# A second DMA queue for later weights and tokens, and a new instruction order, in an attention and feed-forward kernel

## The chip, the cores and the metric

The kernel runs on one core of one Trainium2 chip. The metric is the device time of one execution in microseconds, as the median of several executions. The engines are called by the profile's names: PE (TensorE, matrix products), DVE (VectorE), ACT (ScalarE), POOL (GpSimd) and SP (SyncE, which only issues DMAs here). A DMA is issued by an instruction on SP, POOL or ACT, and its packets are moved by 16 DMA engines. Packets of SP's issues show as queue q1 (hardware), those of POOL's as queue q0 (software).

## The reference

Eight batches of 512 tokens with 8 heads of 64, and 32 state rows per batch and head. Tokens read the state and the state reads the tokens, each by attention; both results together (544 rows of 512 for each batch, 4352 rows in all) go through a feed-forward layer with a gate.

```python
scores  = scale * x @ state.T;  a  = softmax(scores);   xread = a @ state
scores2 = scale * state @ x.T;  a2 = softmax(scores2);  sread = a2 @ x
z = concatenate([xread, sread], axis=2)          # (8, 8, 544, 64), then rows of 512
h = z @ w_in                                     # w_in 512 x 2048
g = h * clip(h + 3, 0, 6) / 6
out = g @ w_out                                  # w_out 2048 x 512
```

The weights arrive in eight bytes per number; the kernel loads them so and puts a 32-bit number together from the two halves.

## The kernel before

**Units and steps.** The feed-forward layer is cut along its width of 2048 into 16 tiles of 128, numbered 0 to 15. A *unit* is one pass of eight tiles over one batch, and each tile in it is a *step*. The first sweep takes tiles 0 to 7: units 0 to 7 for the batches' tokens, unit 8 for the state rows of all batches (`sread`). The second sweep takes tiles 8 to 15: unit 9 for the state rows, units 10 to 17 for the tokens. A step makes `h` for its tile (`first(n)`, tile `ps_h`), ACT and DVE turn it into `g` (L1286, L1289), split it into a high and a low part (`g_hi` on ACT, `g_lo` on DVE, L396 and L397) and PE adds three products of them to the accumulators (`second(n)`, tiles `acc`). Products are made of such high and low parts throughout, so that three fast products stand for one exact one. The first sweep's partial output is written to `out` in HBM (`put_out`, L1350); in the second sweep it is added there by an accumulating DMA from POOL (L1176).

**The attention of the next batch** is spread over the steps of the current unit. For batch b its state is loaded by POOL in four block DMAs (`load_state`, L547), its tokens are loaded a second time in a block order that makes DVE's 32 x 32 transposes into a full one (`load_turned`, L611, 16 issues of 512 pieces for each batch, on SP), and a third time by rows (`load_x`, L582, tile `xb`, four issues of 1024 pieces of 256 bytes, on SP). The softmax of the states is moved between partitions by 16 small DMAs (`weights_moved`, L964, "raw<-raw", on SP). PE reads `xb` and the moved weights in `tokens_read` (L992). There is one `xb` buffer, so a batch's tokens go in after the batch before has been read. POOL also stores each batch's attention weights for the second sweep (`keep`, L1387, L1391).

**Weights.** `weight(kind, k, ...)` loads w_in or w_out tile k (L473), ACT converts the upper halves to `tops` (L484, L486), DVE joins the halves (L491), and for w_out ACT and DVE split the result (L518, L520). Tiles 0 to 7 are loaded at the head. Tiles 8 to 15 are loaded one at a time into `raw`, a ring of three buffers that the turned tokens and the moves use as well; the second sweep is the first to use them. All these loads are issued by SP.

**What sets the order.** Every instruction is entered into a `Plan` with its engine, a cost, its readers and writers. `Plan.order` places all of them with a list scheduler that takes, on each engine, the instruction with the smallest number in `RANKS` among those that could start within 0.3 us; the code is then issued in that order, and each engine works through its own list in order. So an instruction that waits holds up whatever stands behind it on its engine. Of a DMA the plan takes the transfer at 330 bytes per ns over one channel, a landing time of 1.4 us and an allowance `late`:

```python
done = channel + self.LANDING + late
...
def Q(rank, size, do, reads=(), writes=(), after=(), pieces=128, cost=0.46, late=2.0):          # SP
def by_pool(rank, size, do, reads=(), writes=(), after=(), pieces=128, cost=1.3, late=3.0):     # POOL
...
for f in range(FPS, NF):                      # tiles 8 to 15
    told = 16.0 + 5.0 * (f - FPS)             # the step from which the load is entered
    weights.append((told, "in", f, 1, ("raw", ("in", f)), told + 4, told + 4))
    weights.append((told + 2, "out", f, 1, ("raw", ("out", f)), told + 6, told + 6))
```

`first_of[n]` is the plan's number of the first product of step n; other entries use it as "not before step n".

Of the kernel before, what the change touches and what calls it, by code (L numbers as in the profile page):

```python
# [17 lines left out]
ALU = mybir.AluOpType  # L18
# [255 lines left out]
def tile_state_attention_then_hardswish_ffn(  # L274
# [87 lines left out]
    def by_pool(rank, size, do, reads=(), writes=(), after=(), pieces=128, cost=1.3, late=3.0):  # L362
        return plan.add("P", cost, rank, do, reads, writes, after, size, pieces, late)
# [211 lines left out]
    def load_x(b, rank, after=(), read=False):  # L575
# [3 lines left out]
        if b:  # L579
            for j in range(J):  # L580
                def load(j=j):
                    nc.sync.dma_start(x_tile(b, read)[:, :, j, :], x_v[b, j])  # L582
# [975 lines left out]
```

## Time and profile before

| what | value |
|---|---|
| median of 3 runs | 650.12 us (648.83 to 651.21) |
| the profiled execution | 647.97 us, of which the span from first to last instruction is 646.2 us |
| PE busy | 633.2 us (98%) |
| DVE busy | 509.9 us (79%) |
| ACT busy | 326.2 us (50%) |
| POOL busy | 53.5 us (8%) |
| granted clock of PE | 1.000 over the whole span |
| packets of SP's queue | 133248, 46.47 MB, 31.1% of 16 engines' span |
| packets of POOL's queue | 9328, 25.63 MB, 16.1% |

The profile is of one execution, so its rows add up to its own time and not to the median. Times in rows are microseconds from the span's start unless marked ns. A matrix product is shown from its start to its end, and products overlap: the next starts 0.23 us after one that is shown as 0.39 long. So PE counts as busy while one is in flight, and an idle gap in the rows is shorter than what the stop costs. "<-" after an idle time names what ended it, by the semaphores' events.

### The profile page before, as it was taken

How to read it: one execution, taken by the hardware profiler on the slowest of the kernel's cores; microseconds unless marked ns; L12 is line 12 of the kernel's file. 1: busy time of each engine (PE TensorE's matmuls, PEld its weight loads, DVE VectorE, ACT ScalarE, POOL GpSimd, SP SyncE). 2: the span in 40 equal slices, each digit the busy share in tenths (PEclk: the TensorE clock that was granted, in tenths of full speed). 3: DMA queues.
4: the chain of work that ended last, by engine and by line, in shares of the span. 5: the costliest groups of instructions: out<-in, count | busy, mean ns of one | idle time of the engine just before them, and what ended most of it. 6: DMA issues, size and time to landing. Idle time of an engine off the chain costs nothing.

```text
span 646.2 us, 11490 instructions
## 1 busy us (share of the span) xinstructions
PE 633.2 (98%) x4444; PEld 518.2 (80%) x4444; DVE 509.9 (79%) x937; ACT 326.2 (50%) x587; POOL 53.5 (8%) x82
## 2 busy tenths in 40 slices
PE   8999989999999999999999999999999999999997
PEld 6566667877776868778899878898989898998996
DVE  5989679888977869786578758888787887897773
ACT  5966444654645454535446545455454364445431
POOL 2200202011020201001000000000000000000000
PEclk9999999999999999999999999999999999999999
DMA  8994796958659478344201031241433341341232
GB/s 295 309 210 92 196 181 148 228 129 188 149 126 209 112 212 172 105 77 146 67 22 66 2 106 66 33 102 23 96 51 83 49 105 22 85 66 16 46 71 66
DMA packets 142774, 73.09 MB, mean 113 GB/s; under 512 B 120896, under 2 KB 130176, under 8 KB 142592
## 3 DMA queue, kind: packets, MB, share of 16 engines
q1 hardware_dynamic: 133248, 46.47, 31.1%
q0 software_dynamic: 9328, 25.63, 16.1%
q8 instruction: 35, 0.57, 0.4%
q10 hardware_dynamic: 144, 0.26, 0.1%
q14 instruction: 19, 0.16, 0.1%
HBM read 42.45 MB, written 26.21 MB: 106 GB/s over the span
## 4 chain that ended last, share of the span: by engine, by line
PE 85%; DMA 5%; DVE 5%; SPq 2%; ACT 2%; issue 1%; DVEq 0%
PE ps_h L1035 28%; PE acc L1035 27%; PE acc L1147 24%; PE ps_s L624 3%; SPq L611 2%; PE ps_h L624 2%; DMA raw<-raw 1%; DMA raw<-in_moe_w_in_dram 1%; DMA early<-in_moe_w_out_dram 1%; DMA raw<-in_moe_w_out_dram 1%; PE ps_h L992 1%; PE acc L1318 1%; PE ps_s L787 1%; DMA st_raw<-in_state_dram 1%; PE acc L723 0%
## 5 line engine op out<-in xcount | busy, mean ns | idle before, releaser
L1035 PE MATMUL acc<-w_out_hi,g_hi 128*128 128x512 f32 x296 | 117.2, 396 | 0.3 <-ACT g_hi L396 0.3
L1035 PE MATMUL acc<-w_out_hi,g_lo 128*128 128x512 f32 x296 | 115.5, 390 | 1.4 <-DVE g_lo L397 1.3
L1035 PE MATMUL acc<-w_out_lo,g_hi 128*128 128x512 f32 x296 | 115.5, 390 | 0.0
L1147 PE MATMUL acc<-w_out_hi,tmp 128*128 128x256 f32 x360 | 89.1, 283 | 0.0
L1035 PE MATMUL ps_h<-aT_hi,wp_hi 128*128 128x512 f32 (+1 forms) x228 | 84.5, 371 | 1.9 <-DVE ot L397 1.4
L1286 ACT ACTIVATE g<-ps_h,three 128x512 f32<-128x512 f32 (+1 forms) x80 | 50.8, 646 | 64.8 <-PE ps_h L1035 55.3
L1035 PE MATMUL ps_h<-aT_lo,wp_hi 128*128 128x512 f32 (+1 forms) x228 | 82.4, 361 | 0.0
L1035 PE MATMUL ps_h<-aT_hi,wp_lo 128*128 128x512 f32 (+1 forms) x228 | 82.0, 360 | 0.0
L1270 ACT ACTIVATE G<-ps_h,three 128x512 f32<-128x512 f32 x64 | 44.2, 690 | 67.2 <-PE ps_h L1035 65.9
L1035 PEld LDWEIGHTS acc<-w_out_hi,g_hi 128*128 128x128 f32 x296 | 55.6, 188 | 19.3 <-issue 6.7
L1289 DVE SCALAR_TENSOR_TENSOR g<-g,ps_h 128x512 f32<-128x512 f32 (+1 forms) x80 | 49.6, 630 | 26.0 <-ACT g L1286 25.6
L1147 PE MATMUL acc<-w_out_hi,g_hi 128*128 128x256 f32 x240 | 68.4, 285 | 0.0
L1147 PE MATMUL acc<-w_out_lo,g_hi 128*128 128x256 f32 x240 | 67.9, 283 | 0.0
L1147 PE MATMUL acc<-w_out_hi,g_lo 128*128 128x256 f32 x240 | 67.9, 283 | 0.0
L1147 PEld LDWEIGHTS acc<-w_out_hi,tmp 128*128 128x128 f32 x360 | 66.8, 192 | 1.3 <-issue 0.8
L1035 PEld LDWEIGHTS acc<-w_out_hi,g_lo 128*128 128x128 f32 x296 | 55.6, 188 | 14.5 <-DVE g_lo L397 2.7
L1035 PEld LDWEIGHTS acc<-w_out_lo,g_hi 128*128 128x128 f32 x296 | 55.6, 188 | 10.6
L396 ACT CAST g_hi<-g 128x512 fp32r<-128x512 f32 (+1 forms) x74 | 42.3, 584 | 37.3 <-DVE g L1289 19.9
L1272 DVE SCALAR_TENSOR_TENSOR G<-G,ps_h 128x512 f32<-128x512 f32 x64 | 43.8, 685 | 17.6 <-ACT G L1270 17.0
L397 DVE TENSOR_TENSOR g_lo<-g,g_hi 128x512 fp32r<-128x512 f32 (+1 forms) x74 | 46.8, 642 | 13.0 <-ACT g_hi L396 12.1
L1035 PEld LDWEIGHTS ps_h<-aT_hi,wp_hi 128*128 128x128 f32 x228 | 43.1, 189 | 10.9 <-DVE ot L397 2.3
L1147 PEld LDWEIGHTS acc<-w_out_hi,g_hi 128*128 128x128 f32 x240 | 45.9, 191 | 6.7 <-ACT wp_hi L396 1.7
(169 smaller groups left out, 1209.8 us busy)
## 6 DMA issues: line engine op xcount, KB each, us to landing
out_dram<-ot POOLq DMA_DIRECT2D x8, 1024.0 KB, 5.8
out_dram<-ot POOLq DMA_DIRECT2D x15, 512.0 KB, 5.9
raw<-in_x_dram SPq DMA_DIRECT2D x112, 64.0 KB, 3.2
xb<-in_x_dram SPq DMA_DIRECT2D x28, 256.0 KB, 5.0
raw<-in_moe_w_out_dram SPq DMA_DIRECT2D x11, 511.8 KB, 7.1
raw<-in_moe_w_in_dram SPq DMA_DIRECT2D x8, 511.0 KB, 4.6
raw<-raw SPq DMA_DIRECT2D x112, 32.0 KB, 2.0
early<-in_moe_w_in_dram SPq DMA_DIRECT2D x3, 1023.0 KB, 10.3
```

What stands on the lines that cost most here:

```text
L396: first = S_(cost, rank, lambda: nc.scalar.copy(hi(), src()), reads, [writes[0]], after)
L397: V(cost, rank, lambda: nc.vector.tensor_tensor(lo(), src(), hi().bitcast(F32), op=ALU.subtract), [*reads, writes[0]], [writes[1]])
L611: nc.sync.dma_start(t[rows, i].rearrange("t (a c) -> t a c", c=NS), x[b, 4 * g + 2 * i + u, :, k * NS : (k + 1) * NS].rearrange("(a t) c - ...
L624: nc.tensor.matmul(out[u][cols, :], made["stT", b][rows, cols], moving(q)[rows], start=True, stop=True,)
L787: nc.tensor.matmul(out[:, j, q % 2], xT(b, q)[:, j * P : (j + 1) * P], apart[:, q], start=True, stop=True,)
L992: nc.tensor.matmul(bank(pr)[cols, u * D : (u + 1) * D], e2T(b, u)[:, j * P + q * NS : j * P + (q + 1) * NS], x_tile(b, True)[:, NG * q + u ...
L1035: nc.tensor.matmul(ps, l, r, start=start and k == 0, stop=stop and k == n - 1)
L1147: nc.tensor.matmul(out, left(a, l), right(b, r), start=p == 0 and z == 0 and y == 0, stop=p == FPS // 2 - 1 and y == 2, skip_group_check=True)
L1270: S_(0.68, n - 1.5, lambda: nc.scalar.activation(g(), by_pass(), AF.Relu, bias=three, scale=-1.0 if turned_sign(FPS + i) else 1.0), [ps], ...
L1272: V(0.63, n - 1.5, lambda: nc.vector.scalar_tensor_tensor(g(), g(), 6.0, by_pass(), op0=ALU.min, op1=ALU.mult), [ps], [g_key])
L1286: in_turn["g", n] = S_(cost + 0.05, rank, lambda: nc.scalar.activation(g(), bank(ps)[:, :width], AF.Relu, bias=three, scale=-1.0 if turned ...
L1289: V(cost, rank, lambda: nc.vector.scalar_tensor_tensor(g(), g(), 6.0, bank(ps)[:, :width], op0=ALU.min, op1=ALU.mult), [ps], [g_key])
```

## The change

- The loads of weight tiles 8 to 15 are issued by POOL and not by SP, and each gets a condition: not before the first product of the step three before the one at which it is entered. (`first_of` now holds step numbers alone, and is made earlier in the code; the list kept in it under "sums" moves to `sum_of["all"]`.)
- The token loads by rows of batches 1 to 7 (`load_x`) are issued by POOL and not by SP.
- The first sweep's output store of a unit becomes four stores, one for each 128 rows, each waiting for its own part of `ot`. What reads the stored rows later (the accumulating stores, `load_part`) waits for the parts that it needs.
- The plan's cost of a POOL issue goes from 1.3 to 0.65, that of a batch's four state loads from 4.8 to 2.4; a token load on POOL is given 1.5. POOL's weight loads get the allowance `late` of 3.0 where SP's had 2.0.
- `RANKS` is new in full (the list differs in length, as there are more instructions), so the order on every engine can differ anywhere.
- Turned loads, moves, the loads of tiles 0 to 7, of batch 0, and the reloads of the second sweep stay on SP.

```diff
@@ RANKS: replaced in full
...
-    def by_pool(rank, size, do, reads=(), writes=(), after=(), pieces=128, cost=1.3, late=3.0):
+    def by_pool(rank, size, do, reads=(), writes=(), after=(), pieces=128, cost=0.65, late=3.0):
...
-            nc.sync.dma_start(flat[:, :, : flat.shape[2] - 1], src)
+            (nc.gpsimd if k >= FPS else nc.sync).dma_start(flat[:, :, : flat.shape[2] - 1], src)
...
-        Q(load_rank, 524.288 * n, load, writes=[key], pieces=128 * n if kind == "out" else 512,
-          late=2.0 if k >= FPS else 0.5)
+        pieces_of = 128 * n if kind == "out" else 512
+        if k >= FPS:
+            by_pool(load_rank, 524.288, load, writes=[key], after=[first_of[max(first_of) - 2]],
+                    pieces=pieces_of)
+        else:
+            Q(load_rank, 524.288 * n, load, writes=[key], pieces=pieces_of, late=0.5)
...
-        by_pool(rank, 140.0, load_blocks, writes=[key], after=after, pieces=512, cost=4.8)
+        by_pool(rank, 140.0, load_blocks, writes=[key], after=after, pieces=512, cost=2.4)
...
-                    nc.sync.dma_start(x_tile(b, read)[:, :, j, :], x_v[b, j])
-                Q(rank, 420.0, load, writes=[(*key, j)], after=after, pieces=1024, cost=0.55)
+                    nc.gpsimd.dma_start(x_tile(b, read)[:, :, j, :], x_v[b, j])
+                by_pool(rank, 420.0, load, writes=[(*key, j)], after=after, pieces=1024, cost=1.5)
...
-            [*[(*o_key, 2 * q + r) for r in range(2)], ("part", units[k][1])], [], (), 1000.0, 256, 3.0)
+            [*[(*o_key, 2 * q + r) for r in range(2)], *[("part", units[k][1], 2 * q + r) for r in range(2)]], [], (), 1000.0, 256, 3.0)
...
-          [("part", units[k][1])], [("po", k, j) for j in range(2, J)], after, pieces=256)
+          [("part", units[k][1], j) for j in range(2, J)], [("po", k, j) for j in range(2, J)], after, pieces=256)
...
-            by_pool(n + 3, 262.0 * nt, lambda: nc.gpsimd.dma_start(rows_of(b), ot()), keys, [("part", b)], pieces=512)
+            for j in range(nt):
+                by_pool(n + 3, 262.0, lambda j=j: nc.gpsimd.dma_start(rows_of(b)[:, j], ot()[:, j]),
+                        [keys[j]], [("part", b, j)])
```

## Rows read from the trace of the kernel before

**Rows 1.** The windows by stage: the stretch and its length, then for each engine its busy time and its instructions, the granted clock of PE (1.00 is full), the mean busy share of the 16 DMA engines, and GB/s.

```profile
0.00:20.00 20.00, 16.78 (x156) 14.32 (x156) 13.33 (x29) 11.35 (x23) 4.20 (x12) 1.00 0.89 314
20.00:60.00 40.00, 39.05 (x280) 23.17 (x278) 37.69 (x69) 30.09 (x57) 3.86 (x7) 1.00 0.79 180
100.00:200.00 100.00, 99.88 (x698) 77.09 (x697) 86.52 (x158) 53.17 (x93) 13.85 (x24) 1.00 0.70 165
220.00:285.00 65.00, 65.00 (x475) 49.58 (x474) 48.64 (x83) 31.97 (x55) 3.28 (x6) 1.00 0.58 139
390.00:642.00 252.00, 252.00 (x1845) 225.14 (x1829) 199.83 (x376) 119.47 (x224) 17.48 (x15) 1.00 0.31 62
20.00:642.00 622.00, 616.43 (x4290) 503.93 (x4288) 495.86 (x908) 314.88 (x566) 49.26 (x70) 1.00 0.47 107
```

**Rows 2.** The windows of four narrow stretches of the first sweep, in the same columns (PE, its weight loads PEld, DVE, ACT, POOL, clock, DMA share, GB/s).

```profile
56.00:62.00 6.00, 5.14 (x85) 3.83 (x84) 5.97 (x12) 4.64 (x8) 0.74 (x2) 1.00 0.28 64
75.00:83.00 8.00, 6.48 (x96) 3.76 (x94) 5.33 (x9) 3.79 (x6) 0.00 (x0) 1.00 0.42 73
92.00:98.00 6.00, 5.01 (x45) 2.82 (x30) 5.59 (x12) 3.52 (x7) 0.00 (x0) 1.00 1.02 175
205.00:210.00 5.00, 3.58 (x16) 2.64 (x15) 4.77 (x10) 3.36 (x7) 0.00 (x0) 1.00 0.92 149
```

**Rows 3.** The waits of PE between 20 and 646, longest first: the waiting tile and line, what it waited for, us in total, times, longest.

```profile
PE ps_h L1035 <- DVE ot L397: 1.4, 1, 1.4
PE acc L1035 <- DVE g_lo L397: 1.3, 2, 0.9
PE ps_h L992 <- DMA raw<-raw: 0.8, 1, 0.8
...
```

**Rows 4.** Three links of the chain of work that ended last, from the stretches 62 to 97 and 195 to 212: start, us, what.

```profile
69.41 9.22 DMA raw<-raw
84.46 7.09 DMA raw<-in_moe_w_in_dram
...
197.39 5.68 DMA raw<-in_moe_w_out_dram
```

**Rows 5.** The timelines of ACT and DVE at the conversions of three later weights: start, us, engine, line, operation, tiles, and in brackets the engine's idle time before and what ended it.

```profile
75.98 0.78 ACT L486 CAST tops<-raw 128x512 f16<-128x512 bf16 x1 [2.34 <-DMA raw<-in_moe_w_out_dram]
91.58 0.80 ACT L484 ACTIVATE tops<-raw 128x512 f16<-128x512 bf16 x1 [0.85 <-DMA raw<-in_moe_w_in_dram]
203.09 0.78 ACT L486 CAST tops<-raw 128x512 f16<-128x512 bf16 x1 [0.45 <-DMA raw<-in_moe_w_out_dram]
76.79 0.69 DVE L491 SCALAR_TENSOR_TENSOR raw<-raw,tops 128x512 uint32<-128x512 uint32 x1 [2.43 <-ACT tops L486]
```

**Rows 6.** The timeline of PE, in the same columns: the start of step 15, the read of batch 2's tokens, and the stop near 207.

```profile
96.33 0.50 PE L1035 MATMUL ps_h<-aT_hi,wp_hi 128*128 128x512 f32 x1
...
111.96 0.26 PE L992 MATMUL ps_h<-xb,raw 128*32 128x64 f32 x4
...
206.55 0.39 PE L1035 MATMUL acc<-w_out_lo,g_hi 128*128 128x512 f32 x1
206.78 0.39 PE L1035 MATMUL acc<-w_out_hi,g_lo 128*128 128x512 f32 x1
208.59 0.50 PE L1035 MATMUL ps_h<-aT_hi,wp_hi 128*128 128x512 f32 x1 [1.42 <-DVE ot L397]
```

**Rows 7.** The timeline of SP, which issues DMAs: start, us that SP spent on it, tiles.

```profile
68.82 0.54 SPq L473 DMA_DIRECT2D raw<-in_moe_w_out_dram  x1
...
84.46 0.99 SPq L473 DMA_DIRECT2D raw<-in_moe_w_in_dram  x1
...
93.30 0.49 SPq L582 DMA_DIRECT2D xb<-in_x_dram  x1
```

**Rows 8.** The DMA issues of the whole span: tiles, issuing engine, count, KB of each, median us from issue to landing.

```profile
out_dram<-ot POOLq DMA_DIRECT2D x8, 1024.0 KB, 5.8
...
xb<-in_x_dram SPq DMA_DIRECT2D x28, 256.0 KB, 5.0
raw<-in_moe_w_out_dram SPq DMA_DIRECT2D x11, 511.8 KB, 7.1
...
raw<-raw SPq DMA_DIRECT2D x112, 32.0 KB, 2.0
...
out_dram<-ot SPq DMA_DIRECT2D x3, 256.0 KB, 2.9
```

**Rows 9.** POOL's DMA issues by source line: ns that one takes on POOL as least/median/most, first and last start; and from the same view of L1387 the time that POOL sat idle before the keeps and what ended it (us, times). A store of L1350 has 512 pieces (batch 0's 128), a keep of L1387 and a state load of L547 have 128.

```profile
L1350 POOL DMA_DIRECT2D out_dram<-ot x8: 562/767/767, 69.5 to 339.3; - x8
...
L1387 POOL DMA_DIRECT2D a2hi<-aT_hi x1: 555/555/555, 104.0 to 104.0; - x1
...
  ACT aT_hi L396: 166.5, 8
...
L547 POOL DMA_DIRECT2D st_raw<-in_state_dram x28: 552/554/1047, 6.2 to 219.5; - x28
```

**Rows 10.** The first part of the page: busy time, share of the span and instructions of each engine.

```profile
PE 633.2 (98%) x4444; PEld 518.2 (80%) x4444; DVE 509.9 (79%) x937; ACT 326.2 (50%) x587; POOL 53.5 (8%) x82
```

**Rows 11.** The DMA queues between 20 and 60: packets, MB, and the time that their packets took, as a share of 16 engines over the 40 us.

```profile
q1 hardware_dynamic: 18619, 5.99, 70.1%
q0 software_dynamic: 448, 1.18, 8.6%
```

More of the change, by code (lines that the diff above doesn't have):

```diff
@@ L533, in tile_state_attention_then_hardswish_ffn @@
     wp_at, scores_at, turned_first = {}, {}, {}
+    first_of, in_turn = {}, {}
     def load_state(b, rank, after=()):
@@ L1036, in product @@
                 k += 1
-    first_of, in_turn = {}, {}
     whole_of, sum_of = {}, {}
@@ L1097, in quarter_sums @@
         wide, half = (0.34, 0.21) if last else (0.6, 0.34)
-        if "sums" not in first_of:
-            first_of["sums"] = [m for slot, users in plan.users.items() for m in users
+        if "all" not in sum_of:
+            sum_of["all"] = [m for slot, users in plan.users.items() for m in users
                                 if slot[0] in ("ot", "top", "sread", "apart")]
@@ L1103, in quarter_sums @@
             to(0, 2), four()[:, :, 1:3], four()[:, :, 0:1].to_broadcast(list(four()[:, :, 1:3].shape)),
-            op=ALU.subtract), g_keys, [s_keys[0]], first_of["sums"] + chain)
+            op=ALU.subtract), g_keys, [s_keys[0]], sum_of["all"] + chain)
         V(half, rank, lambda: nc.vector.tensor_tensor(
@@ L1161, in seconds @@
         S_(0.36, rank, lambda: nc.scalar.mul(E()[:, left_half], bank(acc[0])[:, left_half], -1.0 / 6.0),
-           [acc[0]], [e_key], first_of["sums"])
+           [acc[0]], [e_key], sum_of["all"])
         def join(cost, out, a, b, reads, writes):
```

205 rows, old and new, of the table RANKS are left out of this document.

## The prediction

> **What bounds the kernel now.** I read the windows first. TensorE (PE) is busy 616.43 of the 622 us between 20 and 642, at full clock throughout [rows 1]; what a change of queues can win there is PE's 5.57 us of idle and what each restart costs. Ahead of 20 PE lacks 3.2 us. From 390 to 642 it is busy 252.00 of 252.00: the second sweep has nothing to win and can only lose. From 20 to 60 VectorE (DVE) is busy 37.7 of 40 us, so what little PE misses there is elementwise work, not a queue.
>
> Then I cut the first sweep more finely to find the idle [rows 2]: 0.86 at 56 to 62, 1.52 at 75 to 83, 0.99 at 92 to 98, 1.42 at 205 to 210; the other 0.78 is spread. The list of who waited for whom names DVE tiles for most of it [rows 3], but DVE is only the last link. The chain of work and the timelines of ACT and DVE show the first link of the three large ones [rows 4, 5]:
> - At 92 to 98 the chain runs through the load of a later w_in tile, issued at 84.46 and 7.09 us under way. ACT's conversion (L484) stands in ACT's order at 91.58 and waits for it; DVE's join, the moves' transposes and then `g_lo` follow, and PE idles 0.99.
> - At 205 to 210 the same with a w_out tile: issued 197.39, 5.68 us, ACT's conversion at 203.09, then a row of DVE work in fixed order, and PE starts at 208.59 after 1.42 [rows 6].
> - At 75 to 83 a w_out tile issued at 68.82 [rows 7] holds ACT for 2.34 (75.98) and DVE for 2.43 (76.79) [rows 5]. Besides, a move raw<-raw issued right behind it on SP, at 69.41, needs 9.22 us where the median is 2.0 [rows 4, 8], and 0.8 us of PE's idle is a wait for such a move [rows 3].
>
> So 1.52 + 0.99 + 1.42 = 3.93 us of idle hang on three of the sixteen loads of weights with number 8 and up. PE wants none of these weights before the second sweep; they hurt because ACT and DVE take their conversions in a fixed order, among work that PE wants now. A stop costs more than its idle: from 206.78 to 208.59 there are 1.81 us between two starts that are 0.23 apart otherwise, so 1.58 is lost for 1.42 idle, 0.16 for the restart [rows 6]. I count five stops at the three places, three of them in the first, 0.8 us. Together **4.7 us**.
>
> **The change, part by part.** *Later weights to GpSimd (POOL).* Sixteen issues leave SP. What matters more is the new condition: a load added at step n may not be issued before the first product of step n-3. With the ranks in the code (16 + 5 per tile, w_out two later) the first may go at step 13, the second only at step 15, the last at step 50. Step 15 starts at 96.33 [rows 6]; today both loads of 68.82 and 84.46 are issued before that [rows 7]. So two of the three guilty loads leave the place where DVE is busy 5.97 of 6 and 5.59 of 6 us [rows 2], and their DVE work, 0.69 for each join [rows 5], with them. It is done later, where DVE is busy 86.5 of 100 and 48.6 of 65 us [rows 1]. The third falls in with a plan that allows a POOL load 3.0 us beyond transfer and landing, where it allowed an SP load 2.0: 1.6 + 1.4 + 3.0 = 6.0 us instead of 5.0, against a median of 7.1 for a w_out tile and the 5.68 of the guilty one [rows 4, 8]. Between no gain (other loads become late instead) and the full 4.7, I take the removal of all three.
>
> *Given back.* Three loads of sixteen stop PE today. In the new order the moved loads meet a DVE as full as at 100 to 200 at first and emptier later; from 220 to 285, where the last of them go, PE is now busy 65.00 of 65.00 with DVE free a quarter of the time [rows 1]. Between none and three new stops, I count one of the mean size, 3.93/3 + 0.16 = **1.5 us**.
>
> *Tokens of batches 1 to 7 to POOL.* 28 issues. On POOL no load of 1024 pieces is shown. The nearest: 128 pieces take 555 ns (keep, L1387) and 512 pieces 767 (store, L1350) [rows 9], 0.55 ns a piece, which makes 1.05 us; bounds 0.55 (as for 128) and 1.53 (in proportion to the pieces). 28 x 1.05 = 29 us, on an engine that is busy 53.5 of 646 us [rows 10] and off the path. What hides a later landing: of batch 2 the last part is issued at 93.30 [rows 7], lands 5.0 us later in the median [rows 8] and is read at 111.96 [rows 6]. That is 13 us of cover; when it is gone, PE waits at L992 for each us beyond. In the DMA engines the loads should become cheaper: between 20 and 60 POOL's queue shows 448 packets [rows 11] for 896 pieces issued there (two keeps of 128, one state of 128, four state loads of 128 each), so it joins small pieces. Its packets took 8.6% of 640 us for 1.18 MB, 47 us a MB, and SP's 70.1% for 5.99 MB, 75 us a MB; 7.3 MB of tokens so cost 343 instead of 548, 13 us of all 16 engines. The moves left on SP gain from that and from no longer queueing behind tokens; I book nothing, as the 0.8 us that PE waits for a move is counted above. Were the small packets of SP and POOL's large ones to get in each other's way instead, the same 13 us of cover stands in front of it.
>
> *Output stores in four parts.* 32 issues of about 0.55 for 8 that take 5.9 in all [rows 9]: 17.6 - 5.9 = 11.7 us more on POOL. A part of 256 KB lands in 2.9 us, the whole in 5.8 [rows 8], so the `ot` tile comes free up to 3 us sooner. No PE wait is put down to a store: worth 0. The finer keys of the accumulating stores, a sweep later, change nothing.
>
> *Cheaper POOL costs and the new order.* Costs of 0.65 and 2.4 are the plan's figures and act through the order alone. Where nothing is idle an order gains nothing; I book 0, with the idle left, 5.57 - 3.93 = 1.6, as the upper bound of a gain. POOL grows by 29 (tokens), 8 x 0.77 + 8 x 0.55 = 10.6 (weights) and 11.7 to 105 us.
>
> Sum: 4.7 - 1.5 = 3.2. The profiled execution took 647.97 with a span of 646.2; it would take 644.8. It lies 2.15 below the median of the three runs, 650.12, and I carry the difference over: **646.9**.
>
> **A rule against it.** POOL's state loads take 552 ns at least and 554 in the median, and 1047 once [rows 9], in stretches in which DVE is busy 87 to 94% of the time [rows 1]. The Trainium skill (SBUF — State Buffer, "SBUF: two separate sides") says that a DVE instruction in a two-port mode locks GpSimd out, so that it can't write descriptors and its DMAs look blocked by DVE. The trace agrees at most in that one issue; were it the rule here, the gain would fall to nothing, by the third rival.
>
> **Rivals.**
> 1. *The stop moves.* Three of the moved loads, or of the moves, stop PE elsewhere: 4.7 - 3 x 1.5 = 0.2 gained, 649.9. For it: a fixed order with a DVE as full as in rows 1 leaves little room. Against: the condition on the steps, and PE without idle from 220 to 285. Chance 0.22.
> 2. *POOL's order blocks: slower.* POOL's keeps of `aT_hi` wait for ACT, 166.5 us in eight waits [rows 9]. A load ordered behind such a wait is as late as ACT is, and its conversion stops ACT and DVE in turn: 1.5 us in each of up to seven batches. From five on (7.5 - 4.7 = 2.8) it is slower, 652.9; with seven, 655.9. Against: tokens are issued 13 us and more before they are read, and the order can place them ahead of the keep. Chance 0.16.
> 3. *POOL's issues stretch.* With 1047 for 554 ns the six moved loads of a unit end 3 us later in turn, and the three stops stay: 650.1. This is what the rule would do. Chance 0.03.
> 4. *More than forecast.* No new stop, and the order takes the remaining 1.6 too: 650.12 - 4.7 - 1.6 = 643.8. Chance 0.09.
>
> **How the numbers follow.** The forecast has 0.50, from no new stop (645.4) to nearly two (648.1); that is its own range. A difference of 0.3%, 2 us, is about what a measurement of this kernel can tell from none. Below 648.2 lie the forecast and rival 4: 0.59 faster. Rivals 1 and 3: 0.25 same. Rival 2: 0.16 slower. The range goes down to 642.0 (all idle of 20 to 642, 5.6, with 1.4 for its restarts, and 1.1 of the 3.2 us at the head) and up to 653.5, which takes in rival 2 with five stops.
>
> **What would show it.** Right: at most one later weight issued before 96; no ACT wait of over 0.5 us for a later weight; PE idle in 20 to 642 down from 5.6 to about 2.5; token loads near 1.05 us each on POOL; POOL near 105 us; far fewer packets on POOL's queue than 28 x 1024 for the tokens. Wrong: PE idle at L992 on tokens, POOL issues of several us, idle after 390, or the same idle behind other DVE instructions.

## The result and the profile after

The changed kernel takes 655.67 us in the median of 14 runs (652.16 to 659.14), the kernel before 650.75 us beside it on the same chip: a ratio of 1.0077, interval 1.0049 to 1.0104. It is slower by 5 us, where 646.9 and faster was forecast. The profiled execution of the changed kernel took 652.16 us, with a span of 650.4. When the changed kernel was timed again beside other experiments, one of ten executions took 2200 us; without it the median of that repeat is 655.35 and not 656.14.

The windows after, in the columns of [rows 1]:

```profile
20.00:80.00 60.00, 59.45 (x442) 39.97 (x441) 52.82 (x95) 38.35 (x69) 14.14 (x23) 1.00 0.74 184
80.00:100.00 20.00, 16.85 (x94) 11.45 (x93) 15.55 (x32) 8.35 (x17) 3.52 (x4) 1.00 0.70 109
100.00:200.00 100.00, 99.25 (x693) 76.82 (x693) 85.32 (x156) 52.08 (x92) 34.46 (x54) 1.00 0.80 182
200.00:220.00 20.00, 14.68 (x81) 9.85 (x80) 11.75 (x20) 7.54 (x13) 1.33 (x2) 0.91 0.45 85
...
390.00:642.00 252.00, 252.00 (x1861) 225.52 (x1861) 203.62 (x383) 121.84 (x228) 17.43 (x15) 1.00 0.30 61
```

PE lacks 0.55 us between 20 and 80, and then 3.15 and 5.32 us in two stretches of 20 us; the second sweep is as full as before. Products counted in the two timelines of PE say the same: the 201st product of 512 columns starts at 81.7 us after and at 85.8 before, so the change is 4.1 us ahead there. At the 701st it is 4.6 behind (223.1 and 218.5), and so it stays to the end. The two orders put the smaller products at different places, so the count is a rough measure: in idle time alone the lead at 80 is 1.3 us (0.55 for 1.84).

The longest wait of PE, which answers to [rows 3], and the longest wait of DVE for a load (us, times, longest):

```profile
PE acc L1041 <- DVE g_lo L398: 8.4, 3, 5.3
...
DVE tmp L720 <- DMA raw<-in_x_dram: 10.8, 4, 7.0
```

DVE's timeline at the two places:

```profile
91.46 0.71 DVE L720 STREAM_TRANSPOSE tmp<-raw 128x512 f32<-128x512 f32 x1 [3.29 <-DMA raw<-in_x_dram]
...
206.66 0.71 DVE L720 STREAM_TRANSPOSE tmp<-raw 128x512 f32<-128x512 f32 x1 [6.96 <-DMA raw<-in_x_dram]
207.30 0.65 DVE L398 TENSOR_TENSOR g_lo<-g,g_hi 128x512 fp32r<-128x512 f32 x1
```

A transpose of the next batch's turned tokens stands in DVE's order ahead of `g_lo`, which PE wants at once. It waits 6.96 us for a load, and `g_lo` waits behind it. The links of the chain of work there (start, us, what), which answer to [rows 4]:

```profile
83.70 7.73 DMA raw<-in_x_dram
...
198.07 8.57 DMA raw<-in_x_dram
```

Both are turned loads, which the change leaves on SP. The timelines of SP and POOL show what was issued beside them:

```profile
78.69 13.79 SPq L617 DMA_DIRECT2D raw<-in_x_dram  x16
80.08 3.52 POOL L588 DMA_DIRECT2D xb<-in_x_dram  x4 [7.96 <-PE ps_h L998]
...
189.70 16.97 SPq L617 DMA_DIRECT2D raw<-in_x_dram  x16
190.77 0.90 POOL L588 DMA_DIRECT2D xb<-in_x_dram  x1 [1.59 <-PE ps_h L998]
196.77 1.76 POOL L588 DMA_DIRECT2D xb<-in_x_dram  x2
```

The tokens now go out while the turned loads do, 1.4 and 1.1 us behind the first of them, as soon as a product (L998) has read the batch before. Beside the second stop POOL also issues one w_in and one w_out tile (188.41 and 196.22) and four small state loads. Before, SP put tokens and turned loads in a row, as its timeline shows:

```profile
190.54 6.17 SPq L611 DMA_DIRECT2D raw<-in_x_dram  x7
...
198.23 0.43 SPq L611 DMA_DIRECT2D raw<-in_x_dram  x1
198.70 5.35 SPq L582 DMA_DIRECT2D xb<-in_x_dram  x4
206.04 4.04 SPq L611 DMA_DIRECT2D raw<-in_x_dram  x8
```

The DMA queues of the changed kernel between 189 and 207 (packets, MB, share of 16 engines), and the landing of turned loads there:

```profile
q0 software_dynamic: 656, 2.16, 51.5%
q1 hardware_dynamic: 7574, 0.94, 45.6%
...
raw<-in_x_dram SPq DMA_DIRECT2D x16, 64.0 KB, 6.5
```

The 16 engines are full, and POOL's queue (q0) has more than half of their time while the urgent loads, on q1, take the rest. Of the 2.16 MB on q0 the tokens are 1.05 and the two weight tiles as much, so this view alone does not say which of them costs; the experiments do.

### The profile page after: what moved, and what is told of

The parts are those of the page before. It is cut to its first block, busy times and chain, and to the rows that moved or that the text cites. A ratio compares the mean times of both kernels' runs of the same rounds, so it can differ in the third digit from the quotient of the medians.

```text
span 650.4 us, 11556 instructions
## 1 busy us (share of the span) xinstructions
PE 633.3 (97%) x4440; PEld 517.9 (80%) x4440; DVE 510.2 (78%) x937; ACT 325.7 (50%) x587; POOL 99.7 (15%) x150
## 4 chain that ended last, share of the span: by engine, by line
PE 82%; DVE 5%; SPq 5%; DMA 5%; issue 1%; ACT 1%; DVEq 0%
PE ps_h L1041 26%; PE acc L1041 25%; PE acc L1152 23%; PE ps_s L630 3%; SPq L970 3%; DMA raw<-in_x_dram 3%; PE ps_h L630 2%; SPq L617 2%; DMA raw<-raw 1%; PE acc L1323 1%; DMA early<-in_moe_w_in_dram 1%; PE ps_h L998 1%; DVE tmp L720 1%; ACT tops L487 0%; DVE nm L897 0%
## 5 line engine op out<-in xcount | busy, mean ns | idle before, releaser
L1181 POOL DMA_DIRECT2D out_dram<-ot x15 | 17.4, 1162 | 275.2 <-DVE ot L1170 275.2
```

Source lines behind the costliest of these rows:

```text
L1181: plan.add("P", 1.3, rank, lambda: nc.gpsimd.dma_start(rows_of(units[k][1])[:, 2 * q : 2 * q + 2], ot_of(k)[:, 2 * q : 2 * q + 2], accum_o ...
```

## The experiments

Each is timed beside the kernel before on the same chip (650.5 to 651.1 us). Two theories stood at the outset. A: the tokens on POOL starve the turned loads on SP. B: the new order itself is at fault.

**Parts undone, one at a time.** Changed kernel; the first with the tokens' line back on SP, the second with the weights' line, the third with both:

```diff
-  nc.gpsimd.dma_start(x_tile(b, read)[:, :, j, :], x_v[b, j])
+  nc.sync.dma_start(x_tile(b, read)[:, :, j, :], x_v[b, j])
...
-  (nc.gpsimd if k >= FPS else nc.sync).dma_start(flat[:, :, : flat.shape[2] - 1], src)
+  nc.sync.dma_start(flat[:, :, : flat.shape[2] - 1], src)
```

> The changed kernel with the token loads of batches 1 to 7 issued by SP again, at the places that the new order gives them; everything else as changed. Theory A (POOL's packets of up to 4 KB and more share the DMA engines with SP's turned loads of 128-byte packets; a turned load beside them lands after 7 to 9 us, and the DVE transposes stop PE): the two stops behind L720 (2.7 and 5.3 us) go or shrink to under 1.5 together, DVE's waits for turned loads fall from 10.8 to under 4 us, and the time falls by 4 or more to 649 to 652. Theory B (the new order itself asks for the turned loads too early, whoever carries the tokens): the waits stay at 8 or more and the time at 654 to 658.

> The changed kernel with the loads of weights 8 to 15 issued by SP again, new order kept. Theory A: tokens stay on POOL beside the turned loads, so most of the lateness stays; 0.5 MB a weight now queues in front of turned loads on SP instead: 653 to 657. Theory B: also about 655, since the order is unchanged. This run separates the two parts of the move, not the theories.

> The changed kernel with tokens and weights both issued by SP again, new order and four-part stores kept. Theory A: with only stores and keeps left on POOL in the first sweep, turned loads land as before (median 3 to 4 us): 648 to 652. Theory B: 655 or more, because the order was made for two queues and now everything waits in one.

Measured: tokens on SP 645.76 us, ratio 0.9937 (0.9902 to 0.9972), faster than both kernels and than the 649 to 652 of theory A; weights on SP 654.07, 1.0063 (1.0041 to 1.0085); both on SP 650.01, 0.9998 (0.9967 to 1.0030). The new order and the four-part stores alone are worth nothing, so B falls in its plain form. Under this order, with the tokens on SP, the weights on POOL gain 650.01 - 645.76 = 4.2 us in the medians (2.4 to 3.2 when like executions are compared, as the last section shows), and with the weights on POOL the tokens there cost 655.67 - 645.76 = 9.9. Taken the other way round, the tokens on POOL cost 654.07 - 650.01 = 4.1 with the weights on SP, and the weights on POOL then gain nothing: 655.67 with them, 654.07 without, and the intervals of the two ratios overlap. So the effects do not add in this order.

**The same parts alone, in the old order.** Kernel before with only the tokens' line on POOL, only the weights' line, or both (the edits above, turned round).

> The kernel before, in its own order, with only the issue of the token loads of batches 1 to 7 moved to POOL. Theory A: turned loads issued beside the tokens land later (median from 3.2 to over 4 us), DVE's waits for them rise from 1.9 to 6 or more, and the time rises by 2 to 6 us to 653 to 657. Theory B: within 2 us of the kernel before, 649 to 652.

> The kernel before, with its own order and whole stores; only the weight loads from number 8 on are issued by POOL. Theory A (what costs time is the tokens' large packets beside SP's turned loads; the weights on POOL help): between 645.5 and 648.5 us for 650.8 before, as the weights were worth 4.2 us in the new order (650.01 against 645.76); ACT's waits for w_in and w_out under half of the 12.1 us of before. Theory B (POOL's queue hurts whatever it carries): 652 or more, with DVE waiting for turned loads (L714) more than 4 us. Theory C (the weights are worth something only in the new order): 649 to 651.

> The kernel before, with its own order and whole stores; both the weights from number 8 on and the tokens of batches 1 to 7 are issued by POOL. If the two effects add as they do in the new order (weights -4.2, tokens +9.9 to +12.1): 656 to 659 us. If the new order of the changed kernel had taken back part of the tokens' price, this kernel is slower than the changed one's 655.7 by 2 us or more. If they do not add, since SP's queue is freed of both: 651 to 655.

Measured: tokens 662.90, ratio 1.0198 (1.0154 to 1.0242), more than either theory had; weights 649.04, 0.9994 (0.9971 to 1.0016); both 650.14, 0.9998 (0.9964 to 1.0033). The tokens alone cost 12.1 us, which speaks against B. But it is not the wait that A named: DVE waits 3.0 us for turned loads, where A had 6 or more. Of the other two, the weights came out as theory C had it, and both together as none of the three expectations did: the effects do not add here either, and in the old order both parts together cost nothing. The waits of ACT in the run with the tokens alone name what was late there:

```profile
ACT tops L484 <- DMA raw<-in_moe_w_in_dram: 14.2, 2, 7.2
```

There the w_in loads, still on SP and behind turned loads that crawl, are late: the one issued at 84.24 lands after 12.45 us, where the kernel before took 7.09 [rows 4]. With the weights on POOL too, this victim is gone. So the tokens on POOL slow whatever SP's queue holds then, and the order decides whether somebody waits for it. DVE's timeline in the run with both shows the old order's choice:

```profile
217.35 1.28 DVE L714 STREAM_TRANSPOSE tmp<-raw 128x512 f32<-128x512 f32 x2
```

The old order asks for batch 6's turned tokens at 217.35, and there they wait for nothing; the new one asked at 206.66 - 6.96 = 199.70, when the last load of that transpose was 1.63 us old (198.07). In the numbers by which `Plan.order` places things (no times of the chip), that load stands 23.9 us ahead of the transpose in the old order and 5.2 in the new. At the first stop these times are alike (6.3 and 6.4 us). What differs at both is how many loads the first transpose must wait out: in the old order it needs the 4th and the 5th of the batch's 16 turned loads, in the new one the 9th and the 11th.

**Is it POOL's packets or any second queue?** Changed kernel with the tokens on ACT's queue, which moves them in packets of 256 bytes (29264 packets for 7.60 MB; the same loads add 2240 packets to POOL's queue); and a kernel of DMAs alone.

```diff
-  nc.gpsimd.dma_start(x_tile(b, read)[:, :, j, :], x_v[b, j])
+  nc.scalar.dma_start(x_tile(b, read)[:, :, j, :], x_v[b, j])
```

> The changed kernel, but the tokens of batches 1 to 7 are issued by ACT's queue instead of POOL's: still another queue than SP's, at the same time as the turned loads, but in packets of 256 bytes rather than POOL's 4096. Theory A1 (the size of the other queue's packets starves SP's packets of 128 bytes): the turned loads land near 4 us in the median, DVE's wait for them under 3 us, total 645 to 650 (ACT pays 28 issues of some 0.05 to 0.1 us, and what it queues behind them). Theory A2 (any second queue beside the turned loads starves them): DVE waits 7 us or more, 654 to 658. Theory A3 (ACT's order suffers: its token issue waits for the buffer that TensorE frees, and the work behind it on ACT is late): over 652 with waits of PE on ACT's g_hi and little wait of DVE for turned loads.

Measured: 656.73 us, ratio 1.012 (1.0061 to 1.0179). DVE's wait:

```profile
DVE tmp L720 <- DMA raw<-in_x_dram: 13.3, 4, 6.3
```

As slow as with POOL, and DVE waits as long for turned loads: A1, which blamed the size of POOL's packets, falls, and A2 holds in the main. A3 may have a share that was not separated: ACT stands 5.0 us before two `g_hi` until a token load lands, and an issue takes ACT 0.37 us at least, not 0.05 to 0.1. The kernel of DMAs alone:

```python
def phase(b, beside, tiles):    # DVE writes a corner of every tile: all loads start together
    for t in (turned[0][:, 0, 0:2], turned[1][:, 0, 0:2], *tiles):
        nc.vector.memset(t, 0.0)
    beside()                    # nothing; tokens on POOL, ACT or SP; two w_out tiles on POOL or ACT
    load_turned(b)              # the 16 turned loads of a batch on SP
    close(...)                  # DVE reads a corner of every tile
```

> A kernel that leaves out the whole computation and writes zeros: eight phases, each the 16 turned loads of one batch on SP (1 KB rows of 128-byte packets), released together with one other set of loads: 0 nothing, 1 tokens on POOL, 2 tokens on ACT, 3 tokens on SP behind nothing, ahead of the turned loads, 4 two w_out tiles on POOL, 5 two w_out tiles on ACT, 6 tokens on POOL again, 7 nothing again. Time from the first issue to the last landing of the turned loads. Theory A1: phases 0 and 7 about 12 to 14 us (16 issues of some 0.6 us and a landing of 3), phases 1 and 6 at least 4 us more, phase 2 less than 2 us more, phase 4 up to 4 us more. Theory A2: phases 1, 2, 4, 5, 6 all at least 3 us more. If the cost needs the rest of the kernel (theory D: the starving comes from moves and other traffic): all phases within 2 us of phase 0. Times of whole phases say nothing on the kernel before.

Its windows for phase 0 (nothing beside), 1 (tokens on POOL), 2 (on ACT) and 4 (w_out on POOL); the columns after the length are DVE, POOL, clock, DMA share and GB/s:

```profile
23.20:31.60 8.40, 0.44 (x6) 0.00 (x0) 1.00 0.64 106
31.70:44.80 13.10, 0.34 (x3) 3.65 (x4) 1.00 0.96 161
45.00:57.10 12.10, 0.40 (x3) 0.00 (x0) 1.00 1.03 169
...
70.10:81.50 11.40, 0.34 (x3) 1.11 (x2) 1.00 0.83 183
```

From first issue to last landing the turned loads took 10.1 us alone (10.0 in the last phase), 14.6 and 14.1 beside tokens on POOL, 14.0 beside ACT's, 13.1 beside w_out tiles on either queue. Behind tokens on SP itself it is 14.1 from the first token issue, 11.0 from the first turned one. The phases overlap by 1.3 to 1.7 us, as DVE releases the next one before the last load has landed. So 1 MB more costs 3 to 4.5 us whoever issues it, as A2 had it, and D falls; the 12 to 14 us expected of the phases alone were too many. The DMA engines are full beside tokens on POOL and ACT (0.96 and 1.03, alone 0.64) and busy 0.83 beside the w_out tiles.

**Only the moment.** Tokens of batches 2 and 5 alone, which stand beside the turned loads at the two stops: first held back on POOL until the last turned load of the next batch has landed, then put back on SP. The changed kernel ran once more beside them.

```diff
+  go = lambda: nc.gpsimd.dma_start(x_tile(b, read)[:, :, j, :], x_v[b, j])
+  held_back.append(go) if b in (2, 5) else go()
...
+  if b in (3, 6) and asked[b] == 16:          # the last turned load of that batch
+      nc.gpsimd.tensor_copy(corner[rows], t[rows, i, 0:2])
+      while held_back: held_back.pop(0)()
```

```diff
+  (nc.sync if b in (2, 5) else nc.gpsimd).dma_start(x_tile(b, read)[:, :, j, :], x_v[b, j])
```

> The changed kernel, tokens still on POOL, but those of batches 2 and 5 (the two that stand beside the turned loads at the two stops of 80 to 100 and 200 to 220) are held back: POOL first copies a corner of the last turned load of the next batch, so it waits for its landing. One copy of 32x2 more for each. Theory T (what costs is the moment: the order wants the turned loads some 10 us after their first issue, and the tokens take DMA time just then): DVE's wait for turned loads falls from 10.8 to under 3 us, total 644 to 648 against 655.7. Rival L (tokens held back are late in turn): PE waits at the token products (L998) or ACT behind it, 650 or more. Rival N (the other batches' tokens or the weights are to blame): the waits stay above 7 us, 654 to 657.

> The changed kernel, but the tokens of batches 2 and 5 alone are issued by SP again, the other five batches' stay on POOL. Theory T: nearly all of the 9.9 us between the changed kernel and the one with all tokens on SP (645.8) is won, 645.5 to 648.5; DVE's wait for turned loads under 3 us. Rival N (each batch's tokens cost their share): 2 of 7 of the 9.9 us are won, about 652.8.

> The changed kernel once more, beside the two above on the same chip: 654 to 657 us, with DVE's wait for turned loads (L720) near 10.8 us.

Measured: held back 646.15 us, ratio 0.9928 (0.9891 to 0.9964); two batches on SP 646.46, 0.9933 (0.9898 to 0.9968); the changed kernel again 656.14, 1.0074 (1.0045 to 1.0103). With the tokens held back, POOL's timeline, and the windows of the two stretches in the columns of [rows 1]:

```profile
94.49 0.64 POOL L629 COPY corner<-raw 32x2 f32<-32x2 f32 x1 [17.19 <-DMA raw<-in_x_dram]
95.07 3.52 POOL L591 DMA_DIRECT2D xb<-in_x_dram  x4
...
206.24 0.18 POOL L629 COPY corner<-raw 32x2 f32<-32x2 f32 x1 [6.15 <-DMA raw<-in_x_dram]
206.76 0.90 POOL L591 DMA_DIRECT2D xb<-in_x_dram  x1 [0.34 <-issue]
```

```profile
80.00:100.00 20.00, 20.00 (x181) 14.23 (x180) 16.66 (x33) 9.17 (x17) 4.10 (x5) 1.00 0.57 107
200.00:220.00 20.00, 20.00 (x110) 14.52 (x109) 17.84 (x34) 10.54 (x19) 5.69 (x9) 1.00 0.56 134
```

Same queue, same packets, some 15 us later (95.07 for 80.08, 206.76 for 190.77): the 8.47 us of idle are gone, DVE's wait for turned loads is 2.2 us, and PE waits for no token. With two batches on SP that wait is 4.2 us, above the 3 expected, and PE still waits 1.8 us for `g_lo`. Nearly all of the 9.9 us hang on two batches of seven, and on their moment. Of the profiled executions, the changed kernel (652.16) and the one with two batches on SP (644.25) start their 201st products together, at 81.7 and 81.6. At the 251st they are 2.6 us apart, at the 601st 2.8, at the 701st 8.0, and 7.9 at PE's last product.

**The stores.** Changed kernel and order, the eight stores of the first sweep whole again, each at the place of its last part.

```diff
-  by_pool(n + 3, 262.0, lambda j=j: nc.gpsimd.dma_start(rows_of(b)[:, j], ot()[:, j]), ...
+  by_pool(n + 3, 262.0, lambda j=j: store(j), ...     # store() issues dma_start(rows_of(b), ot()) at the fourth call
```

> The changed kernel in its own order, but each of the eight output stores of the first sweep is issued as one DMA again, at the place of its last part. If the new order is what makes the tokens on POOL cost (its 5.2 us between the issue and the wanted time of batch 6's turned loads), nothing changes: 654.5 to 657.5 for 655.7, DVE's wait for turned loads over 8 us. If the four-part stores carry the difference between the changed kernel and the kernel before with both loads on POOL (650.1): 649 to 651.5.

Measured: 658.54 us, ratio 1.0107 (1.0046 to 1.0168), a little above the expected 654.5 to 657.5, with the interval reaching into it; DVE waits 12.7 us for turned loads. So the four-part stores do not carry the difference to the 650.14 of the old order with both loads on POOL. What is left is the order, through which alone the plan's new costs act too.

## Why the prediction was wrong, step by step

**The step that failed** is the tokens' part, in its sentence on what hides: "Were the small packets of SP and POOL's large ones to get in each other's way instead, the same 13 us of cover stands in front of it." The 13 us cover the tokens. What was got in the way of were the turned loads, which stay on SP and had been booked at nothing, and they have no such cover: at 88.2 and 199.70 DVE asks for loads that land at 91.4 and 206.6. So I looked for the price at the transfer that was moved and not at the transfers beside which it was put. Its term was 0; measured it is 9.9 us (645.76 to 655.67) with the weights on POOL as in the change, and 4.1 with them on SP. The kernel before had shown the lack of cover already, in DVE's timeline:

```profile
89.36 0.71 DVE L714 STREAM_TRANSPOSE tmp<-raw 128x512 f32<-128x512 f32 x1 [1.88 <-DMA raw<-in_x_dram]
```

I had also put SP's relief down on the side of gains, though at nothing: the tokens no longer stand ahead of other things in its queue. Near the second stop that queue was what kept the tokens behind the first half of the turned loads.

The Trainium skill (DMA: Bandwidth & Descriptors, "Issuing engines are not separate DMA queues") says that DMAs issued by SP, ACT and GpSimd run on the same 16 engines and interleave, and that issuing from several saves the issuer's time alone. The phases beside tokens on POOL and ACT agree, 14.0 to 14.6 us for 10.1, and so does the one behind tokens on SP, 14.1 with the tokens' own issues. I did not weigh this rule; it speaks against the change.

**The order was booked at 0, and with the four-part stores alone it is 0** (650.01). But its transposes want the 9th and the 11th turned load where the old ones want the 4th and the 5th. What a transfer costs then depends on it: with both loads on POOL the old order takes 650.14, the new one 655.67. The prediction treated the order and the queues as terms of one sum, and they are not.

**The weights: near in size with the tokens out of the way, but the reason is not shown.** 4.7 - 1.5 = 3.2 was forecast, and 4.2 measured in the new order with the tokens on SP; in the change itself, with the tokens on POOL, they gain nothing (655.67 for 654.07). In the old order the gain is not measurable either (649.04 for 650.52). POOL issues two of the loads at 69.14 and 81.74 there, nearly where SP did [rows 7], and still PE's stops near 95 and 207 are gone. Others have come in their place, between 100 and 200, one of them behind a w_out load for which ACT waits. The windows, in the columns of [rows 1], and ACT's timeline:

```profile
80.00:100.00 20.00, 19.94 (x179) 14.02 (x167) 17.84 (x35) 9.99 (x19) 1.51 (x2) 1.00 0.97 165
100.00:200.00 100.00, 96.81 (x681) 74.40 (x681) 83.75 (x152) 51.40 (x89) 18.55 (x32) 1.00 0.71 170
200.00:220.00 20.00, 20.00 (x113) 15.23 (x112) 18.03 (x33) 10.52 (x19) 3.91 (x8) 1.00 0.66 150
...
155.29 0.78 ACT L486 CAST tops<-raw 128x512 f16<-128x512 bf16 x1 [5.06 <-DMA raw<-in_moe_w_out_dram]
```

That is rival 1, the stop that moves, in the old order. The gain needs the new order; whether through the condition on the steps or through the rest of it was not tested alone. In the changed kernel only one later weight is issued before 96, at 71.36, and ACT's waits for later weights fell from 12.1 us (7.9 for w_out, 4.2 for w_in) to this row, which is two waits where none over 0.5 us was forecast:

```profile
ACT tops L487 <- DMA raw<-in_moe_w_out_dram: 3.0, 2, 1.8
```

With the tokens out of the way the forecast of 646.9 lies beside 645.76, 646.15 and 646.46. That is closer than its working: with the tokens on SP, PE still idles 3.9 us between 20 and 642, where about 2.5 was forecast.

**POOL's times** were nearly right. Busy time on the page is 99.7 us for 105, and the views of POOL's issues by source line (least/median/most ns) give 0.89 us for a token load, where 1.05 was taken:

```profile
L588 POOL DMA_DIRECT2D xb<-in_x_dram x28: 882/886/907, 56.8 to 289.6; - x28
```

So rival 3, stretched issues, is out, and with it the prediction's "rule against it" as a price here. Rival 2 named the right sign and, by luck, a size near it (655.9 with seven batches), but not the cause: the loads behind the two stops are SP's, and none of POOL's waits for ACT stands ahead of them. The range ended at 653.5, since it took its upper end from rival 2 with five stops; what cost most was not among the rivals.

## What to carry to other kernels

Moving a transfer to another queue did not give it other DMA engines here; it took away the order in which one queue served them. Before such a move, list the transfers that will now run beside it, find who asks for each of them and how soon after its issue, and hold the patient transfer back behind the urgent one: one small copy that waits for the urgent load was worth 10 us here. Keep the part that gains, here the weights, which gain only with the tokens out of the way; and test each part alone and with the others, since the same two loads on POOL cost nothing in one order and 5 us in another.

## What the runs showed of the hardware

**A long stop also costs clock.** PE's timeline of the changed kernel around the stop of 5.32 us, and the windows behind it:

```profile
202.30 0.39 PE L1041 MATMUL acc<-w_out_lo,g_hi 128*128 128x512 f32 x1
208.00 0.80 PE L1041 MATMUL acc<-w_out_hi,g_lo 128*128 128x512 f32 x1 [5.32 <-DVE g_lo L398]
208.59 0.63 PE L1041 MATMUL acc<-w_out_hi,g_hi 128*128 128x512 f32 x1
209.02 0.63 PE L1041 MATMUL acc<-w_out_lo,g_hi 128*128 128x512 f32 x1
```

```profile
207.90:210.00 2.10, 2.00 (x4) 1.17 (x4) 1.94 (x5) 1.89 (x3) 0.00 (x0) 0.50 0.01 1
210.00:212.50 2.50, 2.50 (x34) 0.59 (x33) 2.47 (x4) 0.00 (x0) 0.00 (x0) 0.74 0.00 0
```

After the stop the granted clock is 0.50, the level of 1.2 GHz, and products start 0.43 us apart instead of 0.23. 2.10 x 0.50 + 2.50 x 0.26 = 1.7 us are lost on top of the idle. The stop of 2.70 us before 93.40 cost no clock: behind it the clock is 1.00, and from 93.74 on products start 0.24 us apart. The prediction's 0.16 us for a restart had been read from a stop of 1.42 us [rows 6].

**The first microseconds differ between executions.** Timelines of PE, the same 16 products in the kernel with held-back tokens and in the one with two batches on SP:

```profile
8.90 3.51 PE L802 MATMUL ps_s<-sread_t,w_in 128*128 128x64 f32 x16
```

```profile
8.20 1.97 PE L793 MATMUL ps_s<-sread_t,w_in 128*128 128x64 f32 x16 [0.26 <-DVE sread_t L783]
```

In the first they go at half the pace, though the clock column reads 1.00 in both; by the 51st product of 512 columns this has cost 4.7 us (43.9 and 39.2). It is not the edit: the times of the first kernel lie at 645.1 to 646.9 and at 650.2 to 650.4, and its profiled execution is one of the latter; the profiled one with all tokens on SP (649.11) starts at half the pace too. So a median depends on how many executions of either kind are in it. With all tokens on SP seven of ten times lie at 644.7 to 647.3, with tokens and weights on SP five of ten at 646.1 to 648.5. Between the medians of these groups the weights gain 2.4 us and between those of the other executions 3.2, where the medians of all give 4.2; that the groups are the two ways to start is likely, but not shown for each time. Of the tokens' 9.9 us most stays: lowest against lowest time it is 7.5 us, highest against highest 8.8. Why an execution starts in one way or the other is open.
